# Output sums of the last products in four seats of a free buffer, and the planner's traced prices kept to the end

## The chip, the cores and the metric

The kernel runs on one core of one Trainium2 chip. The metric is device time in microseconds: 1794.24 us is the median of three runs of the kernel before (1792.06 to 1795.07). One further execution was profiled. TensorE (PE) does the matrix products and has a second stream for loading weights (PEld); VectorE (DVE), ScalarE (ACT) and GpSimd (POOL) do the rest; SyncE (SP), ACT and POOL issue DMAs. Each engine works through its own instructions strictly in the order in which the program lists them, so an instruction that waits holds up everything behind it on its engine.

## The reference

Two attention layers, A (32 heads, 8 keys at a dilation of 2) and B (32 heads, a causal window of 256 keys), each with its own input, weights and output projection; the two outputs are concatenated.

```python
qkv = (x @ wqkv).reshape(B, S, 3, H, Dh)          # S = 2048, D = 1024, H = 32
# A: 8 gathered keys per row, softmax, weighted sum of v
# B: masked scores (0 <= i - j < 256), softmax, weighted sum of v
a = o_A.reshape(B, S, D) @ wo_A
b = o_B.reshape(B, S, D) @ wo_B
return jnp.concatenate([a, b], axis=-1)
```

Everything is float32 outside the kernel. Inside, each large product is made of three products of a rounded part and a remainder (`TERMS`), so the operands are first split in two: ACT or DVE copies the rounded part (line 276 or 279), DVE subtracts it (line 282).

## The kernel before

**Units and rows of heads.** The 2 x 2048 positions are cut into 8 units of 512. Units 0 to 3 are layer B, units 4 to 7 layer A. For each unit and each of 8 groups of 4 heads there are the projection (`qk`), the attention and, later, the output projection. In layer A the last step of an attention ("values", tile `o`, written by PE) is copied by ACT (line 1333) and stored in DRAM as `od4` to `od7` (line 1338, on SP's queue).

**The last stage.** The output projection of layer A is not one product per unit. Units 4 and 5, and units 6 and 7, are each done with seven products of half size in place of eight (`PRODUCTS`, written here (4,0) to (4,6) and (6,0) to (6,6)), on sums of the operands. A product has four groups (n = 0 to 3) of twelve matmuls 128x512; each group fills one of three banks of PSUM (tile `g`), and it is evicted in line 902 (DVE adds a partial sum) or 922 (ACT, for i = 0). After products i = 1 and i = 4 the eviction makes a finished part of the output, in a tile called `o` in the code: the `ost` pool has one buffer (`NST = 1`), and in two of three cases the buffer that held the window's probabilities (`band`) is used once its attention is over. ACT's queue then issues the store to `outs` (line 908). A new sum in the same buffer has to wait until the store from it has landed.

**The background sums.** The sums of operands for (6,2) onwards need rows of `od6` and `od7`. There is one task for each k = 0 to 3: SP loads both (line 1128, two loads of 512 KB into tiles `r`), DVE makes four additions (line 1133), SP stores the result in `sd` (line 1139). The load of `od7` waits for the store of its last row.

**Who sets the order.** There is no hand-written order here: a planner (`Clock`) keeps a clock for each engine while the program is written, and a step that is to follow something (a task's additions, a store) is put on its engine's list when that clock says that what it needs has come (`defer`). So prices in the planner decide where instructions stand, not when they run. It has two sets of prices. With `ck.traced` false a transfer is put in a single line of transfers with the durations in `MOVE` (a load takes 2.12 and 0.14 after a lead of 1.34 on SP). With `ck.traced` true a 512 KB load costs 1.5 and 0.76 after the same lead, 3.6 in all, and only a transfer on the other kind of queue (POOL against the rest) slows it, to half:

```python
        if self.traced:
            return self.share(eng, start + self.LEAD[eng], *((1.5, 0.76) if kind == "load" else (dur, tail)))
        return self.move(start + self.LEAD[eng], dur, tail)
```

The kernel before switches to the second set at the third projection of unit 4 and back at the first of the last products:

```python
        if name == "g":
            ck.traced = marks[0] <= pos["g"] < marks[1]
```

**The seats.** `pbuf` held layer B's probabilities. In layer A its memory is cut into two "seats" (`seats`), into which SP copies the rows of q and k of one group of heads (line 608, shown as `pbuf<-nat`); the scores of that group (tile `s`) read them. Each seat has room for more than 1024 columns.

## Time and profile before

| | |
|---|---|
| median of 3 runs | 1794.24 us |
| profiled execution, its own time | 1793.36 us |
| span in its profile, first to last instruction | 1791.7 us |
| PE busy | 1771.8 us, 99% |
| DVE, ACT, POOL busy | 72%, 52%, 23% |
| mean granted clock of TensorE | 0.998 |

The span leaves out 1.66 us of the execution's own time. PE is busy nearly throughout, so its few idle stretches, and the stretches where its clock is granted by half, are almost all that another order of the same work can win. The last products run from about 1625 us to the end; their first 50 us overlap the last attentions.

### The profile page before, as it was taken

What the parts mean: (1) busy time and instruction counts of PE and PEld (TensorE: products, weight loads), DVE (VectorE), ACT (ScalarE), POOL (GpSimd) and SP (SyncE); (2) the same over time, 40 slices, a digit from 0 to 9 for tenths busy, and PEclk for the clock granted to TensorE, in tenths of its full rate; (3) what the DMA queues carried; (4) which work ended last, traced back from release to release, by engine and by line L of the source; (5) the groups of instructions that cost most, each with busy time, mean ns of one, the idle gap of its engine ahead of it and who ended that gap; (6) DMA issues with size and microseconds to landing.
All of it is one profiled execution on the core that took longest, in us unless ns stands there. A gap on an engine that the chain in (4) does not pass through costs nothing.

```text
span 1791.7 us, 38433 instructions
## 1 busy us (share of the span) xinstructions
PE 1771.8 (99%) x14496; PEld 1443.6 (81%) x14496; DVE 1295.5 (72%) x2881; ACT 936.3 (52%) x2332; POOL 412.2 (23%) x962
## 2 busy tenths in 40 slices
PE   9999999999999999999999999999999999999999
PEld 7787777888778888878788788888888887887887
DVE  6777876768867769867678556566577869677966
ACT  5565566555656565656554524533354455455442
POOL 3322323222342223332223410100011101001210
PEclk9999999999999999999999999999999999999999
DMA  8355664644656556555556266666576769848984
GB/s 258 105 149 136 186 168 136 170 136 142 186 141 165 151 134 166 154 146 146 147 136 185 61 189 190 199 201 202 171 232 207 213 181 290 291 139 274 303 318 143
DMA packets 154793, 324.57 MB, mean 181 GB/s; under 512 B 18032, under 2 KB 58992, under 8 KB 154608
## 3 DMA queue, kind: packets, MB, share of 16 engines
q0 software_dynamic: 45792, 166.74, 30.9%
q1 hardware_dynamic: 98736, 137.02, 26.9%
q10 hardware_dynamic: 10080, 18.35, 2.8%
q8 instruction: 115, 1.88, 0.5%
q14 instruction: 70, 0.57, 0.1%
HBM read 201.33 MB, written 53.48 MB: 142 GB/s over the span
## 4 chain that ended last, share of the span: by engine, by line
PE 94%; DMA 2%; DVE 1%; ACT 1%; issue 1%; SPq 0%; DVEq 0%; ACTq 0%; POOLq 0%
PE g L324 74%; PE s L324 13%; PE o L324 7%; DMA outs<-ost 0%; DMA raw<-sd 0%; ACT s L1400 0%; DMA pbuf<-nat 0%; DVE w L282 0%; DMA raw<-wqk 0%; DMA raw<-xs 0%; DMA qst<-nat 0%; ACT w L276 0%; DVE r L1133 0%; DVE qst L1435 0%; DVE x L282 0%
## 5 line engine op out<-in xcount | busy, mean ns | idle before, releaser
L324 PE MATMUL g<-x,w 128*128 128x512 f32 x3552 | 879.1, 394 | 5.3 <-DVE ost L902 3.5
L324 PEld LDWEIGHTS g<-x,w 128*128 128x128 f32 x3552 | 658.6, 189 | 135.2 <-issue 10.7
L282 DVE TENSOR_TENSOR w<-raw,w 128x512 fp32r<-128x512 f32 x510 | 334.4, 697 | 53.7 <-ACT w L276 47.5
L1395 DVE CUSTOM_DVE_ANT_0 s<-s,mask_d 128x384 f32<-128x384 f32 (+2 forms) x512 | 261.8, 554 | 98.4 <-PE s L324 98.0
L1400 ACT ACTIVATE s<-s,nm 128x384 f32<-128x384 f32 (+2 forms) x512 | 274.4, 537 | 109.9 <-DVE nm L1395 103.3
L324 PE MATMUL g<-w,x 128*128 128x256 f32 (+1 forms) x1728 | 306.3, 327 | 0.5 <-DVE w L282 0.5
L1459 POOL TENSOR_SCALAR_AFFINE_SELECT pbuf<-pbuf 128x128 f32<-128x128 f32 (+1 forms) x605 | 219.8, 391 | 315.8 <-ACT pbuf L1480 313.8
L324 PEld LDWEIGHTS g<-w,x 128*128 128x128 f32 x1728 | 255.5, 190 | 25.2 <-DVE w L282 1.7
L324 PE MATMUL g<-r,w 128*128 128x512 f32 x960 | 238.5, 394 | 0.5 <-DVE r L1359 0.5
L1480 ACT ACTIVATE pbuf<-s 128x384 f32<-128x384 f32 (+2 forms) x480 | 203.4, 504 | 64.7 <-PE s L324 62.1
L324 PEld LDWEIGHTS g<-r,w 128*128 128x128 f32 x960 | 177.4, 188 | 36.0 <-DVE r L1359 1.1
L221 POOL DMA_DIRECT2D raw<-wqk x126 | 68.2, 541 | 389.2 <-DVE w L282 275.1
L324 PEld LDWEIGHTS s<-qst,kst 128*128 128x128 f32 x704 | 113.6, 189 | 42.0 <-ACT s L1400 16.8
L324 PE MATMUL s<-kst,qst 96*128 96x384 f32 (+2 forms) x512 | 142.3, 342 | 0.9 <-ACT s L1400 0.7
L324 PE MATMUL s<-qst,kst 128*128 128x256 f32 (+2 forms) x704 | 137.1, 302 | 4.0 <-ACT s L1400 3.2
L279 DVE CAST w<-raw 128x1024 fp32r<-128x1024 f32 x176 | 121.2, 689 | 8.6 <-PE g L324 7.8
L324 PEld LDWEIGHTS s<-kst,qst 96*128 96x128 f32 x512 | 93.6, 189 | 26.1 <-issue 4.5
L276 ACT CAST w<-raw 128x1024 fp32r<-128x1024 f32 (+1 forms) x80 | 82.4, 1037 | 47.9 <-PE g L324 15.9
L1400 ACT ACTIVATION_READ_ACCUMULATOR s<-s,nm 128x1 f32 x512 | 105.4, 206 | 0.0
L1260 ACT COPY wide<-band 32x512 f32<-32x512 f32 x128 | 79.0, 617 | 29.5 <-DVE band L1251 28.0
L324 PE MATMUL o<-pbuf,vbuf 128*32 128x384 f32 (+2 forms) x1408 | 91.1, 389 | 0.0
L625 ACT ACTIVATE nat<-g 128x512 fp32r<-128x512 f32 x64 | 38.3, 598 | 98.1 <-PE g L324 84.9
(91 smaller groups left out, 1428.1 us busy)
## 6 DMA issues: line engine op xcount, KB each, us to landing
raw<-wqk POOLq DMA_DIRECT2D x126, 512.0 KB, 4.7
raw<-wv POOLq DMA_DIRECT2D x60, 512.0 KB, 4.9
qst<-nat SPq DMA_DIRECT2D x96, 256.0 KB, 5.3
kst<-nat SPq DMA_DIRECT2D x96, 256.0 KB, 5.8
raw<-wo POOLq DMA_DIRECT2D x44, 512.0 KB, 4.5
raw<-xs POOLq DMA_DIRECT2D x28, 512.0 KB, 4.5
outs<-ost ACTq DMA_DIRECT2D x39, 256.0 KB, 3.1
kst<-halo SPq DMA_DIRECT2D x72, 128.0 KB, 4.5
```

What stands on the lines that cost most here:

```text
L221: (self.nc.scalar if early else self.nc.gpsimd).dma_start(raw if len(ap.shape) == 2 else raw.rearrange("p (a b) -> p a b", a=2), ap)
L276: nc.scalar.copy(t[:, 0, :], raw)
L279: nc.vector.tensor_copy(t[:, 0, :], raw)
L282: nc.vector.tensor_tensor(t[:, 1, c:c + 512], raw[:, c:c + 512], t[:, 0, c:c + 512].bitcast(F32), op=ALU.subtract)
L324: nc.tensor.matmul(out, left, right, **k)
L625: nc.scalar.activation(hl[:, 0, :], ps, AF.Copy, scale=sc)
L1260: nc.scalar.copy(diag[r:r + 32, :, :, c:c + 32], turned[r:r + 32, :, :, 1, :])
L1395: nc.vector.tensor_tensor_reduce(ps[:, :n], ps[:, :n], mask[:, cut:full], scale=-1.0, scalar=BIG, op0=ALU.add, op1=ALU.min, accum_out=nm)
L1400: nc.scalar.activation(ps[:, :n], ps[:, :n], AF.Exp, bias=nm, scale=-1.0, accum_out=sm)
L1459: nc.gpsimd.affine_select(w, w, pattern=[[0, m], [step, n]], compare_op=ALU.is_ge, fill=0.0, base=base, channel_multiplier=chan)
L1480: nc.scalar.activation(w, ps[:, :pack * n].rearrange("p (j n) -> p j n", j=pack), AF.Exp)
```

## The change

It does two things, both in the last stage.

First, where the output sums of i = 1 and i = 4 are put. They no longer take the `ost` buffer or a `band` buffer in turn. Once the scores of the last group of heads are written (`U * NG - 1 in done["scores"]`), the seats in `pbuf` hold nothing that is needed, and four pieces of 512 columns in them are used in turn.

Second, the planner's second set of prices: it is no longer switched back at the first of the last products (`marks[1]` is gone), but kept to the end.

```diff
             if i in (1, 4):
                 for f in list(going.values())[:-1]:
                     f()
                 where_o["ot"] += 1
-                b = where_o["ot"] % 2
-                o = band[b][:, 1024:1536] if where_o["ot"] % 3 and U * NG - 2 + b in done["o"] else stp.tile([P, S], F32, tag="ost", name="ost")
+                if U * NG - 1 in done["scores"]:
+                    b, at = where_o["ot"] % 2, where_o["ot"] // 2 % 2 * S
+                    o = seats[:, b, at:at + S]
+                else:
+                    o = stp.tile([P, S], F32, tag="ost", name="ost")
...
         if not marks and p[1:] == (DU, 2) and p[0] == "qk":
-            marks.append(len(gemm))
-        if len(marks) == 1 and p[0] == "p":
             marks.append(len(gemm))
...
         if name == "g":
-            ck.traced = marks[0] <= pos["g"] < marks[1]
+            ck.traced = marks[0] <= pos["g"]
```

Lines behind 923 have numbers three higher in the changed kernel: the background additions of line 1133 are its line 1136.

**Where instructions moved.** Up to the last attentions' final steps no engine's list changes. The first place is on DVE, about 1639 us in the profile, just behind the four additions that take the scores of the last group of heads (`band<-s,near`). Before:

```order
L1251 STREAM_TRANSPOSE band<-band 128x1024
L902 TENSOR_TENSOR ost<-g,r 128x512
L1224 TENSOR_REDUCE nm<-band 128x16
L1226 TENSOR_TENSOR band<-band,nm 128x16x40
L282 TENSOR_TENSOR x<-raw,x 128x512 x4
L902 TENSOR_TENSOR ost<-g,r 128x512
L282 TENSOR_TENSOR w<-raw,w 128x512 x2
L902 TENSOR_TENSOR ost<-g,r 128x512
L282 TENSOR_TENSOR w<-raw,w 128x512 x2
L1133 TENSOR_TENSOR r<-r 128x512 x4
L902 TENSOR_TENSOR band<-g,r 128x512
```

Now:

```order
L1254 STREAM_TRANSPOSE band<-band 128x1024
L1136 TENSOR_TENSOR r<-r 128x512 x4
L902 TENSOR_TENSOR pbuf<-g,r 128x512
L1227 TENSOR_REDUCE nm<-band 128x16
L1229 TENSOR_TENSOR band<-band,nm 128x16x40
L282 TENSOR_TENSOR x<-raw,x 128x512 x4
L902 TENSOR_TENSOR pbuf<-g,r 128x512
L282 TENSOR_TENSOR w<-raw,w 128x512 x2
L902 TENSOR_TENSOR pbuf<-g,r 128x512
L282 TENSOR_TENSOR w<-raw,w 128x512 x2
```

The four evictions of product (4,1) go to `pbuf` in place of `ost`, `ost`, `ost`, `band`; and the additions of the second background task, which stood behind the third of these evictions, stand ahead of the first.

The second place is on DVE one product pair later, at the evictions of product (4,4). Before:

```order
L902 TENSOR_TENSOR band<-g,r 128x512
L282 TENSOR_TENSOR x<-raw,x 128x512 x4
L902 TENSOR_TENSOR ost<-g,r 128x512
L282 TENSOR_TENSOR w<-raw,w 128x512 x2
L902 TENSOR_TENSOR band<-g,r 128x512
L1133 TENSOR_TENSOR r<-r 128x512 x4
```

Now:

```order
L902 TENSOR_TENSOR pbuf<-g,r 128x512
L282 TENSOR_TENSOR x<-raw,x 128x512 x4
L902 TENSOR_TENSOR pbuf<-g,r 128x512
L1136 TENSOR_TENSOR r<-r 128x512 x4
L282 TENSOR_TENSOR w<-raw,w 128x512 x2
L902 TENSOR_TENSOR pbuf<-g,r 128x512
```

The additions shown are not the same ones: before they are the third task's, now the fourth's. The third task's have moved up to the end of product (4,2), and the fourth's, which stood in the middle of product (4,6), are here, ahead of the split of the first weights of product (4,5).

The third place is SP's list, its last entries (`od_101` and `od_102` are od6 and od7, `sd_104` is sd6). Before:

```order
L1338 DMA od_102<-r 128x512
L1139 DMA sd_104<-r 128x2x512 x2
L1128 DMA r<-od_101 128x2x512
L1128 DMA r<-od_102 128x2x512
L1139 DMA sd_104<-r 128x2x512 x2
L1690 UNCONDITIONAL_BRANCH
```

Now:

```order
L1142 DMA sd_104<-r 128x2x512 x2
L1341 DMA od_102<-r 128x512
L1131 DMA r<-od_101 128x2x512
L1131 DMA r<-od_102 128x2x512
L1142 DMA sd_104<-r 128x2x512 x2
L1691 UNCONDITIONAL_BRANCH
```

The store of the last attention's rows stands behind the third task's two stores, which wait for its additions; it stood ahead of them. The last two loads follow it in both.

Two smaller moves: the last attention's values stand 27 matmuls earlier among PE's products (behind 69 of them in place of 96), and in product (6,0) three input splits and two weight splits have their rounded part copied by DVE (line 279) in place of ACT (line 276).

## The prediction

> **What bounds the kernel now.** I read the page first, then the waits of PE, then the time line around the one long wait, engine by engine.

> ```profile
> PE 1771.8 (99%) x14496; PEld 1443.6 (81%) x14496; DVE 1295.5 (72%) x2881; ACT 936.3 (52%) x2332; POOL 412.2 (23%) x962
> ```

> PE is the bound, and the change takes no matmul away. Only what PE loses between matmuls can be won or lost. In the waits of PE from 1450 us on, one entry stands out:

> ```profile
> PE g L324 <- DVE ost L902: 3.5, 1, 3.5
> ```

> PE's own time line shows where it lies, and the chain of waits shows how fast PE goes when nothing stops it:

> ```profile
> 1647.58 1.31 PE L324 MATMUL o<-wide,vbuf 128*32 128x8 f32 x40
> 1648.82 0.96 PE L324 MATMUL g<-x,w 128*128 128x512 f32 x3
> 1653.30 7.11 PE L324 MATMUL g<-x,w 128*128 128x512 f32 x24 [3.52 <-DVE ost L902]
> 1660.76 1.62 PE L324 MATMUL g<-x,w 128*128 128x512 f32 x6 [0.35 <-DVE band L902]
> ...
> 1676.68 1.11 PE o L324 x40
> 1677.80 109.76 PE g L324 x483
> ```

> The last row gives 109.76 / 483 = 0.227 us for a matmul 128x512, with no wait in 110 us. From 1648.82 to 1660.76 PE does 3 + 24 of them in 11.94 us where 27 x 0.227 = 6.13 would do. **The loss of the old arrangement is 5.8 us.** The two waits explain 3.87 of it. The rest is the clock; the windows of PE show it (busy, then the granted clock), here and at an earlier pause of 1.37 us that ends at 1501.7 (its row first):

> ```profile
> 1501.68 0.58 PE L324 MATMUL s<-pbuf 32*32 32x40 f32 x41 [1.37 <-issue]
> ...
> 1499.00:1502.00 3.00, 1.63 (x126) 1.00 0.65 154
> 1503.00:1506.00 3.00, 3.00 (x9) 0.50 1.05 352
> 1650.00:1653.00 3.00, 0.00 (x0) 0.97 0.11 44
> 1653.00:1656.00 3.00, 2.70 (x7) 0.50 0.47 175
> 1656.00:1657.00 1.00, 1.00 (x5) 0.89 0.74 143
> ```

> After the pause the clock is at half for about 3.4 us (all of 1653 to 1656 and some tenths on both sides), of which PE works 2.9: 1.5 us lost.

> Why PE waited is in DVE's rows and one of ACT's:

> ```profile
> 1640.21 0.69 DVE L902 TENSOR_TENSOR ost<-g,r 128x512 f32<-128x512 f32 x1 [0.95 <-PE g L324]
> 1640.82 0.81 DVE L1224 TENSOR_REDUCE nm<-band 128x16 f32<-128x640 f32 x1
> 1641.66 0.82 DVE L1226 TENSOR_TENSOR band<-band,nm 128x640 f32<-128x640 f32 x1
> 1642.40 2.49 DVE L282 TENSOR_TENSOR x<-raw,x 128x512 fp32r<-128x512 f32 x4
> 1652.46 0.69 DVE L902 TENSOR_TENSOR ost<-g,r 128x512 f32<-128x512 f32 x1 [7.57 <-DMA outs<-ost]
> 1653.07 1.28 DVE L282 TENSOR_TENSOR w<-raw,w 128x512 fp32r<-128x512 f32 x2
> 1655.35 0.69 DVE L902 TENSOR_TENSOR ost<-g,r 128x512 f32<-128x512 f32 x1 [0.99 <-DMA outs<-ost]
> 1657.15 2.86 DVE L1133 TENSOR_TENSOR r<-r 128x512 f32<-128x512 f32 x4
> 1659.93 0.68 DVE L902 TENSOR_TENSOR band<-g,r 128x512 f32<-128x512 f32 x1
> ...
> 1645.62 0.34 ACTq L908 DMA_DIRECT2D outs<-ost  x1
> ```

> The second eviction of product (4,1) wants the only `ost` buffer, whose store was issued at 1645.62 and took until 1652.4. DVE stands 7.57 us, and PE runs out of banks.

> **Part one: the four seats.** They remove that wait. The first store no longer gates the second eviction; the fifth sum, the first to come back to a used seat, is a product (4,4) sum some 30 us later, against a store that took 6.8 us, so the seats add no wait. Their first use needs the rows that SP put there and the scores that read them, both earlier on their own engines. Taken alone this part would win up to 5.8 us. No operation is added or taken away.

> **Part two: the prices.** They move the background additions ahead of evictions, and these additions wait for loads. The second task's four additions are now DVE's first work after the transposition, before 1640.21. What they need is the load of `od7` rows, on SP's list at the same place in both kernels, and every engine's list is the same up to here, so I take its time from the trace:

> ```profile
> L1128 SPq DMA_DIRECT2D r<-od x1: 567/567/567, 1636.6 to 1636.6; - x1
> ...
> DMA to landing us min/median/max: 9.5/9.5/9.5
> ```

> It lands at 1636.6 + 9.5 = 1646.1. The planner's new prices have 3.6 us for it. So DVE stands from about 1639.3 to 1646.1 in front of the additions; they take 2.86 (the row above), so the first eviction of (4,1) starts at 1649.0 and ends at 1649.7. Queued behind are the three other evictions, the maxima of the last attention and the splits for (4,2).

> PE meanwhile: with three banks, the group n = 3 of (4,1) needs the bank of n = 0. Nine of its twelve matmuls stand ahead of the 40 of 1647.58, so it started at 1647.58 - 9 x 0.227 = 1645.5. Now it starts at 1649.75. **A new wait of 4.2 us**, long enough to bring the half clock, which I price at 1.5 as before (the 3.4 us of it overlap the pause more or less: 0.9 to 1.7). New loss 5.7. Bounds for it: landing one us earlier or later, and the clock's bounds, 4.1 to 7.

> Behind it DVE has no wait left before PE needs the next banks: 0.81 + 0.82 + 2.49 and then three evictions, four halves of weights (2 x 1.28), the sums of the last attention (as long as its maxima) come to about 9.6 us from 1649.7, so the last eviction of (4,1) ends near 1659.3, while PE comes to it at 1660.5. **Term one: 5.7 - 5.8 = -0.1 us.** One wait is exchanged for another of its size.

> **The third task** now stands at the end of (4,2). DVE gets there at about 1668.4: from 1659.3 it has four evictions, two pairs of weight halves, the splits of 2.49, the scaling (as the subtraction, 0.82) and the transposition of 1.24 before it. Its last load can be issued once the store of od7 before it has landed; the values for that store now end near 1654, so with a copy and a store of some 5 us (below) near 1660. Such a load took

> ```profile
> L1128 SPq DMA_DIRECT2D r<-od x1: 1326/1326/1326, 1662.3 to 1662.3; - x1
> ...
> DMA to landing us min/median/max: 10.4/10.4/10.4
> ```

> or, in the rows here, 7.7 and 9.5, so it lands at 1667.7 to 1670.4: DVE stands 0 to 2 us, and PE, whose next bank was evicted just before, has about 1 us of cover. **Term two: +0.3** (0 to 1).

> **The fourth task** stands behind the second eviction of (4,4), where DVE arrives near 1684 (PE ends that group 24 matmuls, 5.5 us, before it comes to (4,5), and the eviction takes 0.69), and ahead of the split of (4,5)'s first weights. SP's list decides when its load lands. The last rows of od7 are now stored behind the third task's two stores, so not before those additions end, 1668.4 + 2.86 = 1671.3 or up to 2 us later; I take 1672. Such a store took 2.0 us alone and 8.6 among others:

> ```profile
> L1338 SPq DMA_DIRECT2D od<-r x1: 337/337/337, 1654.2 to 1654.2; - x1
> ...
> DMA to landing us min/median/max: 2.0/2.0/2.0
> ...
> L1338 SPq DMA_DIRECT2D od<-r x1: 592/592/592, 1628.0 to 1628.0; - x1
> ...
> DMA to landing us min/median/max: 8.6/8.6/8.6
> ```

> It goes behind two stores of half a MB, so I take the middle, 5.3, and for the load 9.1, between these rows' 7.7 (the same pair's other half) and 10.4:

> ```profile
> L1128 SPq DMA_DIRECT2D r<-od x1: 1117/1117/1117, 1661.0 to 1661.0; - x1
> ...
> DMA to landing us min/median/max: 7.7/7.7/7.7
> ```

> It lands at 1672 + 5.3 + 9.1 = 1686.4. Additions 2.86 and half of a weight split (0.69) later, at about 1690.0, PE can go on with (4,5). PE gets there 120 matmuls and 40 small ones after 1660.5: 27.3 + 1.1, so 1688.9. Wait 1.1 us; bounds from the rows: 1672 + 2.0 + 7.7 gives none, 1672 + 8.6 + 10.4 = 1691.0 gives 5.7. For the clock I take 0.9: the pause of 1.37 us at 1501.7 was followed by a half clock (1.7 us at most), and I find no other wait of PE between 1.1 and 3.5 us behind the kernel's first microseconds. **Term three: +2.0** (0 to 7.4).

> [...]

> **What else moved** costs nothing that I can find. In (6,0) DVE makes three copies of 512 and two of 1024 columns that ACT made, some 2.6 us by its own rows; PE waited for nothing there and the splits are made a product ahead. The last attention's values move ahead of 27 matmuls; it is the same work on PE. Uncovered, the copies would cost their 2.6.

> ```profile
> L279 DVE CAST w<-raw 128x1024 fp32r<-128x1024 f32 x4 | 2.7, 678 | 0.0
> L279 DVE CAST x<-raw 128x512 fp32r<-128x512 f32 x4 | 1.6, 412 | 0.4 <-PE g L324 0.4
> ```

> **Sum.** -0.1 + 0.3 + 2.0 = +2.2 us on the profiled span of 1791.7, so 1793.9, and with the 1.66 outside the span 1795.6. The profiled execution (1793.36) is 0.88 under the median of the runs, so the forecast for the median is **1796.4 us**, 0.12% slower. A measurement of this kernel can tell about 0.2% (3.6 us) from no change; its three runs spread over 0.17%. So the likeliest outcome is one that does not stand out.

> **Rivals.** (1) *The change does what it says.* The loads land before DVE reaches the additions, the old wait is gone and none follows: -5.8 and some tenths for the third task, 1789 us. For it: DVE's wait in `ost` and its cause are plain, and the seats do remove it. Against: the 9.5 us row, with lists that are the same up to there; the load would have to land by 1642 for it, 4 us sooner. 12%.

> (2) *The fourth load decides: slower.* The last store of od7 takes its 8.6 behind the third task's stores, the load its 10.4; it lands at 1691.0, PE waits 5.7 us for the weights of (4,5) and the clock falls for 1.7 more. Sum -0.1 + 0.3 + 7.4 = +7.6, 1801.8 us. It is slower by over 0.2% once the load lands after about 1687, with a third task that costs its 1 us a little sooner. For it: nothing that SP issues in these 15 us is alone, POOL has its loads for (4,4) and (4,5) out, and the trace has loads like this of 9.5, 10.4 and, once, 15.9. Against: the 2.0 us row. 40%.

> ```profile
> L1128 SPq DMA_DIRECT2D r<-od x2: 894/1083/1272, 1691.7 to 1692.7; - x2
> ...
> DMA to landing us min/median/max: 15.9/15.9/15.9
> ```

> (3) *The additions aren't what DVE stands at*, the copies in (6,0) lose their cover: -5.8 + 2.6 = -3.2, 1791 us, no change that can be told. 3%.

> The forecast itself, one wait for another with a small one after it, has 45%; its own range is 1792.5 to 1798.5 (term one -1.6 to +1.2, the rest 0 to 3).

> **The numbers.** Faster by over 0.2%: rival 1, 0.12. Within 0.2%: the forecast less its upper edge, and rival 3, 0.45. Slower: rival 2 and that edge, 0.43. The range reaches from rival 1 to rival 2, 1789 to 1802; 2 in 10 is left for a load that lands much sooner or later than any row of this kind.

> **What would show it.** In the profile after: PE's wait of 3.5 on `ost` is gone from the list, no row has `ost`; DVE is idle some 7 us up to 1646 before the additions, the releaser a DMA `r<-od`; PE stops near 1645.5 for about 4 us for a bank, and the granted clock is 0.5 right after. Then DVE is idle again near 1684 to 1686 before the fourth additions, and PE waits near 1689 for a `w` of line 282, between 0 and 6 us. Wrong would be: no idle DVE at 1640 to 1646, or a load that lands by 1642; a PE wait in (6,0) to (6,6), where I expect none; or a time under 1790, which only the absence of the first new wait can give.

## The result and the profile after

| | before | after |
|---|---|---|
| median | 1792.62 us (1792.06 to 1795.07, 7 runs) | 1798.77 us (1796.69 to 1801.89, 7 runs) |
| profiled execution, its own time | 1793.36 us | 1798.03 us |
| its span | 1791.7 us | 1796.3 us |

The ratio is 1.0035, 95% interval [1.0025, 1.0045]: the change makes the kernel slower by 6.2 us in medians. Engine totals say nothing of why; PE is as full as before (engine, busy time, share of the span, instructions):

```profile
PE 1772.7 (99%) x14496; PEld 1442.3 (80%) x14496; DVE 1297.9 (72%) x2886; ACT 934.0 (52%) x2327; POOL 412.1 (23%) x962
```

The waits of PE from 1450 us on (total, times, longest) no longer hold the one on `ost`. Two others stand there:

```profile
PE g L324 <- DVE pbuf L902: 3.7, 1, 3.7
PE g L324 <- DVE w L282: 3.7, 2, 3.4
```

PE's time line puts them at 1646.9 to 1650.6, in front of the group n = 3 of product (4,1), and at 1691.0 to 1694.4, in front of (4,5):

```profile
1650.61 3.17 PE L324 MATMUL g<-x,w 128*128 128x512 f32 x9 [3.73 <-DVE pbuf L902]
...
1694.44 97.77 PE L324 MATMUL g<-x,w 128*128 128x512 f32 x430 [3.44 <-DVE w L282]
```

DVE's time line shows the cause of both. From the transposition on it stands three times before the background additions (line 1136), and each time a DMA lets it go:

```profile
1639.47 1.24 DVE L1254 STREAM_TRANSPOSE band<-band 128x1024 f32<-128x1024 f32 x1
1647.08 2.87 DVE L1136 TENSOR_TENSOR r<-r 128x512 f32<-128x512 f32 x4 [6.38 <-DMA r<-od]
...
1671.31 2.87 DVE L1136 TENSOR_TENSOR r<-r 128x512 f32<-128x512 f32 x4 [2.53 <-DMA r<-od]
...
1690.91 2.87 DVE L1136 TENSOR_TENSOR r<-r 128x512 f32<-128x512 f32 x4 [4.79 <-DMA r<-od]
1693.70 1.29 DVE L282 TENSOR_TENSOR w<-raw,w 128x512 fp32r<-128x512 f32 x2
```

The chain of waits (start, duration, what) names the transfers; the second and third row are the last store of `od7` and the fourth task's load:

```profile
1638.15 8.90 DMA r<-od
...
1675.50 4.35 DMA od<-r
...
1679.87 11.02 DMA r<-od
...
1694.44 97.78 PE g L324 x430
```

The last row also says that nothing holds PE from (4,5) to the end: 97.78 / 430 = 0.2274 us for a matmul. The windows of PE (length, busy time of each engine, then the granted clock, the DMA share and GB/s) show the clock at half behind the first wait and full behind the second:

```profile
1652.00:1655.00 3.00, 3.00 (x37) 2.02 (x39) 3.00 (x6) 0.85 (x2) 0.69 (x2) 0.50 0.94 317
...
1695.00:1698.00 3.00, 3.00 (x15) 2.46 (x14) 3.00 (x6) 0.20 (x1) 1.11 (x2) 1.00 1.03 369
```

One more thing has to be taken off before the two profiles are compared: the transposition, up to which every list is the same, started at 1639.47 in this execution and 1.45 us earlier in that of the kernel before:

```profile
1638.02 1.24 DVE L1251 STREAM_TRANSPOSE band<-band 128x1024 f32<-128x1024 f32 x1
```

So I compare a stretch that both kernels have, whatever came ahead: from the moment PE is ready for the last nine matmuls of product (4,1) in front of the 40 small ones, to its last matmul. It holds 588 matmuls 128x512 and 80 small ones in every kernel. Before, it runs from 1647.58 - 9 x 0.227 = 1645.5 to 1677.80 + 109.76 = 1787.6, 142.0 us; after, from 1650.61 - 3.73 = 1646.9 to 1792.2, 145.3 us. By these two executions the change costs 3.3 us. The medians say 6.2. That gap was the first thing to explain; the other was how the loss divides among the tasks.

### The profile page after: what moved, and what is told of

Its sections match the earlier page's. It is cut to its first block, busy times and chain, and to the rows that moved or that the text cites. A ratio compares the mean times of both kernels' runs of the same rounds, so it can differ in the third digit from the quotient of the medians.

```text
span 1796.3 us, 38445 instructions
## 1 busy us (share of the span) xinstructions
PE 1772.7 (99%) x14496; PEld 1442.3 (80%) x14496; DVE 1297.9 (72%) x2886; ACT 934.0 (52%) x2327; POOL 412.1 (23%) x962
## 4 chain that ended last, share of the span: by engine, by line
PE 91%; DMA 3%; DVE 3%; ACT 1%; issue 1%; SPq 0%; DVEq 0%; ACTq 0%; POOLq 0%
PE g L324 71%; PE s L324 13%; PE o L324 7%; DMA r<-od 1%; DMA od<-r 1%; DMA raw<-xs 1%; DVE w L282 1%; ACT s L1403 0%; DVE x L282 0%; DMA raw<-wqk 0%; ACT w L276 0%; DMA raw<-sx 0%; DVE r L1010 0%; DVE r L1136 0%; DMA qst<-nat 0%
## 5 line engine op out<-in xcount | busy, mean ns | idle before, releaser
L324 PE MATMUL g<-x,w 128*128 128x512 f32 x3552 | 878.2, 393 | 9.1 <-DVE pbuf L902 3.7
L324 PEld LDWEIGHTS g<-x,w 128*128 128x128 f32 x3552 | 657.2, 188 | 138.9 <-issue 6.0
L282 DVE TENSOR_TENSOR w<-raw,w 128x512 fp32r<-128x512 f32 x510 | 334.3, 697 | 47.3 <-ACT w L276 41.0
L324 PE MATMUL g<-w,x 128*128 128x256 f32 (+1 forms) x1728 | 307.1, 327 | 1.9 <-DVE w L279 1.0
L324 PEld LDWEIGHTS g<-w,x 128*128 128x128 f32 x1728 | 255.4, 190 | 27.5 <-DVE w L282 2.5
L324 PE MATMUL g<-r,w 128*128 128x512 f32 x960 | 238.5, 393 | 0.4 <-DVE r L1362 0.4
L324 PEld LDWEIGHTS g<-r,w 128*128 128x128 f32 x960 | 177.3, 188 | 36.0 <-DVE r L1362 1.1
L324 PEld LDWEIGHTS s<-qst,kst 128*128 128x128 f32 x704 | 113.8, 189 | 42.5 <-ACT s L1403 16.8
L324 PE MATMUL s<-kst,qst 96*128 96x384 f32 (+2 forms) x512 | 142.4, 343 | 0.9 <-ACT s L1403 0.7
L324 PE MATMUL s<-qst,kst 128*128 128x256 f32 (+2 forms) x704 | 137.6, 302 | 4.0 <-ACT s L1403 3.2
L279 DVE CAST w<-raw 128x1024 fp32r<-128x1024 f32 x178 | 122.6, 689 | 8.3 <-PE g L324 7.9
L324 PEld LDWEIGHTS s<-kst,qst 96*128 96x128 f32 x512 | 93.7, 189 | 26.3 <-issue 4.5
L324 PE MATMUL o<-pbuf,vbuf 128*32 128x384 f32 (+2 forms) x1408 | 91.1, 388 | 0.0
```

The lines of the kernel that those rows point to most:

```text
L279: nc.vector.tensor_copy(t[:, 0, :], raw)
L282: nc.vector.tensor_tensor(t[:, 1, c:c + 512], raw[:, c:c + 512], t[:, 0, c:c + 512].bitcast(F32), op=ALU.subtract)
L324: nc.tensor.matmul(out, left, right, **k)
```

## The experiments

All times are medians, each kernel beside runs of the kernel before on the same chip: 1792.42 us (25 runs) for e1 to e4, 1792.44 (29) for e5 to e7, 1792.34 (9) for e8 and e9. The edits of e3 to e8 are made in the change. e10 is one execution.

**e1: the seats alone.** The change, with the planner's prices switched back as they were:

```diff
         if not marks and p[1:] == (DU, 2) and p[0] == "qk":
             marks.append(len(gemm))
+        if len(marks) == 1 and p[0] == "p":
+            marks.append(len(gemm))
...
-            ck.traced = marks[0] <= pos["g"]
+            ck.traced = marks[0] <= pos["g"] < marks[1]
```

> The four seats alone, with the planner's prices switched back as in the kernel before. Theory (the moved additions cost the time, the seats win): the additions of the background tasks stand where they stood before, the wait for the ost store is gone, and the loss of 5.8 us at 1649 to 1661 with it: 4 to 6 us under the kernel before, no PE wait over 1 us behind 1630 us. Rival (the seats are worth nothing, since the loads or VectorE's own work end as late as the store): within 1.5 us of the kernel before.

1788.24 us, ratio 0.9971 [0.9960, 0.9981]: 4.2 under the kernel before, as the theory has it. PE's time line from the nine matmuls (they end where the first row starts) to the end:

```profile
1648.24 1.18 PE L324 MATMUL o<-wide,vbuf 128*32 128x8 f32 x40
1649.36 22.09 PE L324 MATMUL g<-x,w 128*128 128x512 f32 x96
1671.38 1.18 PE L324 MATMUL o<-wide,vbuf 128*32 128x8 f32 x40
1672.49 109.81 PE L324 MATMUL g<-x,w 128*128 128x512 f32 x483
```

No row has a wait in brackets. The stretch takes 1672.49 + 109.81 - (1648.24 - 2.05) = 136.1 us, and since 9 + 96 + 483 matmuls at 0.2274 are 133.7 of it and the two rows of small ones nearly all the rest, this is the floor. The seats do what the change says, and this half of it, alone, beats both kernels.

**e2: the prices alone.** The change with the old choice of buffers (`ost` and `band`, the two lines that the diff removes).

> The planner's prices kept to the end, with the old buffers ost and band. Theory: VectorE stands some 6.5 us before the second task's additions, PE stops about 4 us, then the second eviction waits for the first ost store on top (2 to 7 us after its issue), and the fourth task stops PE again: 7 to 13 us over the kernel before, 2 to 6 over the change. Rival (the seats are what costs the time, the order is harmless): no slower than the kernel before.

1799.57 us, ratio 1.0043 [1.0027, 1.0059]: 7.2 over before, as expected, but only 0.8 over the change, where 2 to 6 was expected. The waits of PE:

```profile
PE g L324 <- DVE ost L902: 6.7, 2, 3.6
```

PE's time line has the second of them, and the windows the clock while it lasts:

```profile
1653.42 4.12 PE L324 MATMUL g<-x,w 128*128 128x512 f32 x15
1660.65 15.28 PE L324 MATMUL g<-x,w 128*128 128x512 f32 x54 [3.12 <-DVE ost L902]
```

```profile
1659.00:1660.00 1.00, 0.00 (x0) 0.00 (x0) 0.09 (x1) 0.00 (x0) 0.00 (x0) 0.86 0.95 328
1660.00:1663.00 3.00, 2.35 (x6) 1.86 (x7) 2.96 (x6) 1.99 (x4) 0.53 (x1) 0.50 0.90 308
1663.00:1666.00 3.00, 3.00 (x9) 2.32 (x8) 3.00 (x6) 1.24 (x2) 0.00 (x0) 0.50 0.82 238
```

The first wait, 3.60 us up to 1648.5, is the second task's load (DVE stood 6.44 us for it); this one is a store from `ost` (DVE stood 4.39). The fourth task's additions stand where the change has them and cost nothing here: DVE came to them at 1690.5, 4.4 us later than in the change (1686.1), and did not wait, since after two earlier losses the load was there. The prices alone are as bad as the whole change.

**e3: the fourth task later.** In the change, the planner puts the fourth task's additions 6 us later:

```diff
-        ck.defer(e + (BG_EARLY if key == "s" and who[0] < PAIRS[0] else BG_SLACK), add)
+        late = {(6, 3): 6.0}.get(who, 0.0) if key == "s" else 0.0
+        ck.defer(e + late + (BG_EARLY if key == "s" and who[0] < PAIRS[0] else BG_SLACK), add)
```

> The change, with the fourth background task's additions put 6 us later on the planner's clock; on VectorE they then stand behind the last eviction of product (4,4). Theory: the first new wait (3.7 us and a half clock) stays, the second (3.4 us) goes: 3 to 5 us under the change, so 0 to 3 us over the kernel before. Rival (VectorE has no room there and the wait only moves to the next weight split): within 1 us of the change, some 6 us over the kernel before.

1794.05 us, ratio 1.0004 [0.9996, 1.0013]: 4.7 under the change. One wait is left in PE's list for this stage, the first:

```profile
PE g L324 <- DVE pbuf L902: 3.7, 1, 3.7
```

So the second wait cost 4.7 us in medians, more than twice what was predicted for it, and what remains (the seats' win, the second task's loss) comes out 1.6 us over the kernel before by medians, which the interval does not tell from no change. The theory holds. The profiled execution was the slowest of twelve (1800.19 us), but it had lost that earlier: its nine matmuls in front of the 40 small ones were due at 1652.8, those of the other profiles between 1644.8 and 1647.3.

**e4: all three later.** As e3, with 6 us for the second, third and fourth tasks, `{(6, 1): 6.0, (6, 2): 6.0, (6, 3): 6.0}`.

> The change, with the additions of the second, third and fourth task each put 6 us later on the planner's clock. Theory (only the place of the additions costs): both new waits go and the seats win as in the run with the seats alone: 4 to 6 us under the kernel before. Rival (the new prices cost elsewhere too, such as the splits moved to VectorE in product (6,0)): 2 us or more above the run with the seats alone.

1790.24 us, ratio 0.9988 [0.9978, 0.9997]: better than before, but 2.0 over the seats alone. The waits name one cause:

```profile
PE g L324 <- DVE pbuf L902: 1.0, 1, 1.0
```

The second task's additions now stood behind the second eviction of (4,1), one eviction earlier than in e1, and made the third one late. So the theory's time (4 to 6 under before) missed at 2.2, and the rival's 2 us are met, but not by a cause elsewhere.

**e5: the second task later,** `{(6, 1): 6.0}`.

> The change, with only the second task's additions planned 6 us later; the fourth's stay early. Theory (two separate losses: about 3.7 us of waiting plus some half clock at the second task's additions, about 4.7 in medians at the fourth's): the wait at 1647 to 1650 shrinks to about 1 us, the wait for w near 1691 to 1694 stays at 2 to 5 us; time 2 to 5 us under the change and 1 to 4 over before. Rival (the second task's wait is given back later, since the fourth task then starts no later): within 1.5 us of the change.

1791.00 us, ratio 0.9992 [0.9983, 1.0001]: 7.8 under the change, where 2 to 5 was expected. The wait for `w` did not stay. PE waits less, 22 matmuls further on, and for a bank:

```profile
1691.39 92.77 PE L324 MATMUL g<-x,w 128*128 128x512 f32 x408 [1.52 <-DVE pbuf L902]
```

The reason is the planner again: moving one task had let the fourth slip one eviction down, behind the split that PE had waited for. So e5 moved two things, and neither theory is tested by it; e8 does it cleanly.

**e6: the second task behind the third eviction,** as before and in e1: `{(6, 1): 8.5, (6, 2): 6.0, (6, 3): 6.0}`.

> Second task 8.5 us later, third and fourth 6 us, so that the second task's additions stand behind the third eviction of block (4,1), where before and the seats alone have them. Theory (the 1.0 us wait of TensorE is all that keeps the run with 6 us for each above the seats alone): that wait is gone and the time is 1787.5 to 1789.2, as the seats alone (1788.24). Rival (the new prices cost something elsewhere, such as the splits and copies of the last blocks that moved to VectorE): 1789.7 or more with no wait at the additions.

1789.33 us, ratio 0.9983 [0.9975, 0.9992]. The wait shrank and is not quite gone (a step of the last softmax had moved ahead of the next eviction):

```profile
PE g L324 <- DVE pbuf L902: 0.7, 1, 0.7
```

The time is 0.1 above the theory's range and below the rival's. Of the 1.1 us that are left against the seats alone this wait has 0.7; the rest is below what these medians tell, so neither expectation is borne out in full.

**e7: the second and fourth later, the third left early,** `{(6, 1): 6.0, (6, 3): 6.0}`. (In the text below, "1789.5 to 791 past 1000" is 1789.5 to 1791.)

> Second and fourth task 6 us later, third left early. Theory (the third task's early place costs nothing): as the run with all three 6 us later, 1789.5 to 791 past 1000, that is 1789.5 to 1791.0, and no wait of TensorE near 1671. Rival (the third task's place costs too, by VectorE standing 2.5 us at its load): 1 us or more above that, 1791.3 or more, with a wait of TensorE for pbuf or w between 1668 and 1676.

1789.66 us, ratio 0.9983 [0.9975, 0.9992], in the theory's range. PE has no wait near 1671, though DVE stood 2.16 us at the third task's load; the early place of the third task costs nothing that can be told:

```profile
1667.77 2.87 DVE L1136 TENSOR_TENSOR r<-r 128x512 f32<-128x512 f32 x4 [2.16 <-DMA r<-od]
```

**e8: the second task alone later, the fourth kept in its place.** `{(6, 1): 6.0, (6, 3): -3.0}`; the third and fourth stand among DVE's instructions just as in the change.

> Second task's additions behind the second eviction of (4,1) as in the run before with it alone late; the third and fourth stand exactly where the change has them (the fourth between the second eviction of (4,4) and the split of (4,5)'s first weights, where the run before had let it slip one eviction down). Theory (the fourth load's landing is set by SP's list, near 1687, and TensorE comes to (4,5) earlier by what the second task no longer costs): the wait for w near 1686 to 1691 grows to 4 to 7 us, and the time stands 1 to 5 us under the change, 2 or more over the run in which the fourth slipped (1791.0). Rival (the two losses add up, the fourth's stays 3.4): 1790 to 1792 and a wait of 3.0 to 3.8 for w.

1797.04 us, ratio 1.0034 [1.0021, 1.0048]. The first wait is gone, the second has grown to 4.8. The wait, DVE's row and the two transfers of the chain:

```profile
PE g L324 <- DVE w L282: 4.8, 1, 4.8
```

```profile
1686.39 2.87 DVE L1136 TENSOR_TENSOR r<-r 128x512 f32<-128x512 f32 x4 [6.14 <-DMA r<-od]
```

```profile
1670.43 4.41 DMA od<-r
...
1674.85 11.52 DMA r<-od
```

Wait and time are in the theory's ranges, and the wait is out of the rival's. Four kernels now have the second and the fourth task each in its early and in its late place:

| | fourth early | fourth late |
|---|---|---|
| second early | 1798.77 (the change) | 1794.05 (e3) |
| second late | 1797.04 (e8) | 1789.66 (e7) |

The early place of the second task costs 4.4 us where the fourth is late, and 1.7 where it is early; that of the fourth costs 7.4 or 4.7. So each costs by itself, and by the medians the two do not add. How far they fall short, 2.7 us, is uncertain: the five runs of e8 spread from 1795.35 to 1800.32.

The traces show part of why. Against the change's profile, PE came to (4,5) 5.9 us earlier (1685.1 against 1691.0; 0.8 of it is the earlier start of the stretch). The load came only 4.5 earlier; it did come earlier, since the third task's additions, and SP's list behind them, had moved up too. Of PE's gain 1.3 went into the longer wait, and 1.6 into a half clock that the change's profile does not have at this place (99.39 us for the last 430 matmuls against 97.77). By the profile alone 2.1 us of the first loss were won (7.1 lost in the stretch against 9.2), but against the second profile of the change, e9 below, 5.1. This execution is the fastest of the five, so where the other 1.7 us of the median went is not shown.

**e9: the change once more,** for the clock behind its waits.

> The change itself, once more, for the granted clock behind its two waits of TensorE. Theory (whether the half clock follows a wait of this length is luck of its phase): waits of 3.2 to 4.2 us at the same two places, a half clock of about 3.4 us after the first or the second in some executions and not in others, so that executions spread by 1.7 us or more; time 1797.5 to 1800. Rival (the half clock always follows the first and never the second): the same clock row after both waits as in the profile of the change.

1798.90 us, ratio 1.0043 [1.0030, 1.0055]. PE's two waits are there again, and the windows show the half clock (third number from the right) behind both this time, as the theory allows and the rival does not:

```profile
1648.45 4.21 PE L324 MATMUL g<-x,w 128*128 128x512 f32 x9 [3.64 <-DVE pbuf L902]
...
1693.71 99.39 PE L324 MATMUL g<-x,w 128*128 128x512 f32 x430 [4.08 <-DVE w L282]
```

```profile
1649.00:1652.00 3.00, 3.00 (x8) 2.31 (x7) 2.96 (x6) 1.68 (x2) 0.52 (x1) 0.50 1.03 376
...
1695.00:1698.00 3.00, 3.00 (x9) 2.33 (x8) 2.00 (x4) 0.93 (x2) 0.93 (x2) 0.50 1.10 326
```

By fine windows the first half clock reaches from 1646.8 to 1653.6, twice as long as in the other profile. The stretch takes 1693.71 + 99.39 - (1648.45 - 3.64) = 148.3 us against 145.3: the same kernel, 3.0 us apart, by nothing but the length of two waits and the clock behind them.

**e10: the kernel before once more,** for its own wait.

> The kernel before, once more, for the clock behind its wait for the store. The seats alone won 5.9 us in the profiles from the last three matmuls' place of (4,1) to the end, but 4.2 in medians. Theory (the half clock behind the 3.5 us wait is luck of its phase, and most executions of the kernel before lose less than the 1.5 us that its profile shows there): the wait of 3.3 to 3.7 us is there again, and the clock behind it at 0.9 or more, or half for a shorter part than 2.9 us of work. Rival (the half clock always follows, and the difference lies elsewhere): 0.50 for about 3.4 us again, with the loss of 5.6 to 6.0 us.

1791.61 us, one execution. Both expectations missed. PE did not wait for `ost` at all:

```profile
1649.27 1.18 PE L324 MATMUL o<-wide,vbuf 128*32 128x8 f32 x40
1650.38 6.99 PE L324 MATMUL g<-x,w 128*128 128x512 f32 x27
1659.03 15.90 PE L324 MATMUL g<-x,w 128*128 128x512 f32 x69 [1.66 <-DVE band L902]
...
1675.98 109.82 PE L324 MATMUL g<-x,w 128*128 128x512 f32 x483
```

```profile
1650.43 0.69 DVE L902 TENSOR_TENSOR ost<-g,r 128x512 f32<-128x512 f32 x1 [3.85 <-DMA outs<-ost]
```

The store from `ost` let DVE go 2.0 us earlier than in the profile that the prediction read (1652.46 there), PE came 1.7 us later, and DVE's 3.85 us of standing cost PE nothing at that place; 1.66 came two evictions later, with no half clock behind it (1.00 from 1646 to 1667). PE was late because, just ahead of the stretch, it had stood 1.3 us in short waits before the last scores and then had half clock from 1635.3 to 1638.7. The stretch takes 1675.98 + 109.82 - (1649.27 - 2.05) = 138.6 us: the old arrangement lost 2.5 us here, and 5.9 in the other execution. The whole executions are only 1.75 us apart (1791.61 and 1793.36), since this one had lost most of the difference just before.

All stretches against the 136.1 us of the seats alone, and the medians against its 1788.24:

| kernel | lost in the stretch, by profile | median over the seats alone |
|---|---|---|
| before | 5.9 and 2.5 | 4.2 |
| the change | 9.2 and 12.2 | 10.5 |
| e2 prices alone | 11.9 | 11.3 |
| e3 fourth later | 5.5 | 5.8 |
| e4 all three later | 1.6 | 2.0 |
| e5 second later (fourth slips) | 3.3 | 2.8 |
| e6 second behind the third eviction | 1.0 | 1.1 |
| e7 second and fourth later | 1.3 | 1.4 |
| e8 second later, fourth kept | 7.1 | 8.8 |

The rows agree within 0.6 us except for e8 (1.7), and where two profiles exist their means, 4.2 and 10.7, are close to the medians; with two executions each that is in part chance. So the stretch holds the effect as far as single executions can show it. The 3.3 against 6.2 us at the start came from setting an unlucky execution of the kernel before against a lucky one of the change.

## Why the prediction was right or wrong

The forecast was 1796.4 us and no change that stands out; it is 1798.8, slower, inside the range and 0.3 past the edge of the likeliest case's own. The mechanisms were right at both places. Two sizes were off, one of them that of the kernel before, and the change cost 6.2 us where +2.2 was forecast. That 1796.4 comes as near as 2.4 is luck: it started from 1794.24, the median of three runs, and with seven the kernel before is at 1792.62. From there the same sum gives 1794.8.

**Part one, the seats.** Right: the wait is gone, nothing was added. It is worth 4.2 us in medians, where "up to 5.8" was read from the trace.

**The loss of the old arrangement, 5.8 us.** This is the first step that failed. The sum of rows is correct for the execution that was profiled, but e10 shows 2.5 for the same kernel. What was needed was the loss in the median, 4.2. (Of the 1.9 us that the sum puts down to the clock beside the two waits, the rows give 1.5, as the prediction itself says; the other 0.4 has no row.)

**Term one, -0.1.** The new loss itself was well placed. The load took 8.90 (9.5 predicted), DVE stood 6.38 (6.8), PE waited 3.73 (4.2) and got the half clock behind it; in medians e3 less e1 is 5.8, against 5.7 predicted, though up to 1.1 of it can be other effects of the prices (e6). Only the number that it was set against was too large. By e3 against before, the term is +1.6, within the noise of the two medians.

**Term two, +0.3.** DVE stood 2.53 us at the third task's load, half a us above the bound of 2, and PE did not wait; e7 shows no price. Within its bounds (0 to 1).

**Term three, +2.0.** Mis-sized, and the larger error: 4.7 by the change less e3, and 7.4 by e8 less e7, where PE has lost nothing before it. Its chain was the right one. SP's time line shows the last store of `od7` behind the third task's two stores, as predicted:

```profile
1674.21 0.88 SPq L1142 DMA_DIRECT2D sd<-r  x2
1675.50 0.51 SPq L1341 DMA_DIRECT2D od<-r  x1
```

The store was issued at 1675.5, not 1672. Of these 3.5 us, 1.45 is the later start of this execution; the rest is the third load, which let DVE go at 1671.3 only, and the 1.3 us in which SP issued the two stores ahead; for both the sum had 0.7. The store took 4.35 (5.3 predicted), the load 11.02 (9.1). DVE was free 4.5 us later than predicted, PE at its place 2.1 later, and the wait came to 3.44 for 1.1; in e9 it was 4.08, and the half clock (0.9 predicted) came with it there and not in the other. The upper bound, 7.4, held. The trace had loads of 7.7 to 10.4 in this stage, and the middle of them was taken; here it was 11.02, 11.04 in e9, 11.2 in e5 and 11.5 in e8, all above 10.4. The one longer load that the prediction shows, 15.9, was in its rival and not in its sum.

**What else moved.** Nothing, as predicted: 0.2274 us for each of the last 430 matmuls. What the new prices cost beside the tasks' places is at most the 1.1 us of e6, 0.7 of which is a wait at such a place.

**From the profile to the median.** +1.6 + 0 + 4.7 = 6.3 us agrees with the 6.2 measured, as it must for the first and last, which are differences of medians; that the middle one is 0 is what e7 adds. Rival 1 fell with the load that landed at 1647.1; rival 3 fell with DVE's idle time. Rival 2, the fourth load decides, gave the sign and the place of the last 4.7 us; it put PE's wait at 5.7 with 1.7 for the clock, above what the two profiles show.

**The clock.** The price of 1.5 behind a long pause was right in size (six half clocks lasted 3.41 us, half of it 1.7, and 1.5 where, as in the kernel before, 0.49 us of it lie in the wait), but not in when it comes. In this stretch half clock came with waits of 3.73, 3.64, 4.08, 4.78, 3.75, 3.60 and 3.12 us (the change, e9 twice, e8, e3, e2 twice) and with the 3.52 of the profile before; it did not come with 3.44, 1.66, 1.52 or any shorter. So of these nine waits of 3.12 to 4.78 us eight brought it and one did not; the last section shows how each of them lay. For the short waits the prediction had one case, the 1.37 us at 1501.7, and found no other above 1.1. There is one, of 1.14 us up to 1149.5, and the clock stayed full behind it (1.00 from 1149 to 1160). At the 3.52 us pause the clock fell 3.0 us into it (PE stopped at 1649.78, the clock fell at 1652.81).

## What to carry to other kernels

A planner's price for a transfer sets where the work that needs it stands; with a price of 3.6 us for loads that took 8.9 and 11.0 in the change, that work went in front of things that were ready, and DVE, which ran its list in order, held them all up while it stood 6.38 and 4.79 us. When a wait is priced from one profiled execution, its size is that execution's: take a second one of the same kernel before subtracting (the kernel before lost 5.9 us in one and 2.5 in the other), above all where a half clock may follow or not, as behind the waits of 3.44 and 4.08 us at one place in two executions of the change. And losses in a row at transfers need not add: with the first removed, the second wait grew from 3.44 to 4.78 us here (e8), so try an edit's parts both ways, each alone and each taken out.

## What the hardware showed beside this

**Half clock lasted 3.41 us, or twice that.** By windows of 0.2 us it lasted 3.41 us in six of the eight cases that these profiles show around such waits of PE, and 6.8 in the two others (e9's first wait, e2's second). In those two the clock fell while PE was still idle: in e2 at 1659.7, 2.2 us after PE stopped at 1657.5; in e9 at 1646.8, 2.0 us after 1644.8.

In three profiles two falls were placed in this way. They lie 10.24 us apart in e2 (1649.48 and 1659.72), 47.78 in e9 (1646.81 and 1694.59) and 150.19 in the first profile of the kernel before (1502.62 and 1652.81): 3, 14 and 44 times 3.413 us, each to 0.02. The table is an estimate from these falls and from where PE stops and starts: pieces of 3.413 us are laid over each wait, counted from a fall in the same profile, and PE's idle time is read in the two that the wait reaches into.

| wait of PE | idle in its two pieces | clock falls |
|---|---|---|
| before, 3.52 | 3.03, 0.49 | after the first |
| the change, 3.73 | 1.58, 2.15 | after the second |
| the change, 3.44 | 1.83, 1.61 | not |
| e2, 3.60 | 1.18, 2.42 | after the second |
| e2, 3.12 | 2.18, 0.93 | after the first |
| e3, 3.75 | 1.85, 1.90 | after the second |
| e8, 4.78 | 1.42, 3.36 | after the second |
| e9, 3.64 | 2.00, 1.64 | after the first |
| e9, 4.08 | 1.56, 2.52 | after the second |

**Loads took 8.9 to 11.5 us where the planner had 3.6.** A load of half a MB on SP took 8.9 us at 1638, and 11.0, 11.0, 11.2 and 11.5 us in front of (4,5) in the four profiles in which that load held up DVE (the change, e9, e5, e8). It took 11.2 in e3 and e7 too, where the additions stood later and nothing waited for it. In the change the core's DMA engines were busy for 0.99 of the time from 1675 to 1691. Whether that load would be shorter with less traffic beside it was not tried.
